# Ten exact down chunks instead of eight in two token blocks, and another split of their first parts between VectorE and ScalarE

## The chip, the cores and the metric

The kernel runs on one core of a Trainium2 chip. The metric is the device time of one execution in microseconds (us); the number to compare is the median of several runs.

## The reference

An attention with polynomial sketches is followed by a gated feed-forward block. Cut to what matters:

```python
# attention: batch 4, heads 4, sequence 1088, head size 32, sketch 8 x 8
num = einsum(q_p, einsum(k_p, v));  den = einsum(q_p, sum(k_p)) + 1e-6
x = (num / den) as (4352 tokens, 128)
# feed-forward, 1536 hidden channels
g = x @ w_gate                       # 128 x 1536
val = x @ w_val                      # 128 x 1536
out = (silu(g) * val) @ w_out        # 1536 x 128
```

All inputs come as 64-bit floats; the output is 4352 x 128 in fp32. The change lies in the last product, `@ w_out`.

## The kernel before

**Tiling.** The 1536 hidden channels are 12 chunks of 128 (`NCH`). The 4352 tokens are cut into blocks (L65 to L72): three blocks of the first batch row (384, 320 and 384 tokens), then the later blocks, six of 480 tokens and one of 384. The list of later blocks is `line` (L886), so `line[4]` and `line[5]` are the fifth and the sixth later block, and `line[6]` is the last one (`LAST`). The three first blocks and the attention fill about the first half of the span; the change lies in the second half.

**The loop of the later blocks** (L1405 to L1423) runs over all chunks of all later blocks in one row, 12 turns to a block. This document counts turns within a block: turn t is chunk t. In one turn TensorE gets, in this order: the start of the unit of the next chunk (`start_unit`, two matmuls on L989), the rest of the unit of this chunk (`finish_unit`, four matmuls on L1001 and L1002), and one down product (`down`) of a chunk five turns earlier, taken from the list `todo`.

**A unit** makes gate and value of one chunk. Both products are made in three fast fp32r matmuls each instead of one true fp32 matmul: weights and tokens have been cut beforehand into parts whose products are exact enough together. After the L989 pair, ScalarE scales both sums in place (L992, 960 columns); after the four further matmuls ScalarE makes the silu `sg` (L1004), and VectorE multiplies the value with it into the hidden chunk `hbuf` (L1009). The two sums lie in a pair of PSUM banks; there are three such pairs. The pair is let go at L1012, behind L1009, and the unit that starts three turns after starts in it. Its first L989 writes the bank of the gate, which L1004 has read, its second the bank of the value, which L1009 has read.

**The down product** (L1054) adds hidden chunk times `w_out` chunk into PSUM. For most chunks it is one plain fp32 matmul (L1077, which the profile counts as two records). For the chunks in the list `DOWN` (L888 to L890) it is three fp32r matmuls (L1069, L1071, L1072). For these the hidden chunk has to be cut into three parts as well, by `cut_hidden` (L951):

- `h1`, one turn after the chunk is made: the chunk times a constant, rounded to fp32r. By ScalarE (L968) or by VectorE (L966), as the condition on L965 says. ScalarE does it behind its own work of that turn, VectorE ahead of L1009.
- `h0`, two turns after: chunk minus `h1`, by GpSimd (L969). GpSimd does little else there, so that it starts as soon as `h1` is there.
- `hd`, three turns after: a difference by VectorE (L972), ahead of L1009 of that turn.

The dictionaries `before` and `behind` hold these steps by turn; `finish_unit` runs the first ahead of its matmuls (L998), the second after L1009 (L1013). Within a turn older steps stand first, so VectorE gets L972, then L966, then L1009. Every engine takes its instructions in the order in which the program lists them. There are six sets of the three parts' buffers, taken in turn (L960).

Chunks whose down product stays plain use a copy of `w_out` times -1 (`scaled`), whose places `PLAIN` lists (L887). It is made for chunks 0, 1, 3, 5, 7, 6 and 11; `exchange` (L934), in turn 8 of the sixth block, overwrites those of 1, 5 and 7 with 8, 9 and 10 for the last block.

**Other steps around the change.** In turns 2 and 3 of a block the tokens of the next block are cut: L865 on ScalarE, L868 on GpSimd, L873 on VectorE. In turns 4 to 6 the sums of the block before are brought together and stored: L1095 on ScalarE, L1105 and the transpose L1131 on VectorE, four or more DMAs on SP's queue.

Of the kernel before, what the change touches and what calls it, by code (L numbers as in the profile page):

```python
# [19 lines left out]
def kernel(  # L20
# [796 lines left out]
    def whole(ap):  # L817
        return ap.bitcast(FP32)
# [67 lines left out]
    line = list(range(HEAD, len(blocks)))  # L886
    FINE, PLAIN = range(1, NCH - 1), [0, 1, 3, 5, 7, 6, NCH - 1]  # L887
    DOWN = [(line[2], j) for j in (2, 4, 6, 8, 9, 10)]  # L888
    DOWN += [(i, j) for i in line[3:6] for j in (1, 2, 4, 5, 7, 8, 9, 10)]
    DOWN += [(LAST, j) for j in (1, 2, 4, 5, 6, 7)]  # L890
    down_parts = {}
    h_parts = {}
# [3 lines left out]
    def add_to(where, y, f):  # L896
        where.setdefault(y, []).append(f)
# [53 lines left out]
    def cut_hidden(y, i, j):  # L951

        if not h_sets:
            x = []
            for tag in ("kld", "qld", "vld", "kT", "qT"):
                t = const.tile([P, 2, WB], F32R, tag=tag, name="h" + tag, bufs=1)
                x += [t[:, k, :] for k in range(2)]
            t = const.tile([P, 8, WB], F32R, tag="late", name="hlate", bufs=1)
            x += [t[:, k, :] for k in range(8)]
            h_sets.extend(x[k : k + 3] for k in range(0, 18, 3))  # L960
        n = SPLIT if i == LAST else blocks[i][1]
        h_sets.append(h_sets.pop(0))
        h1, h0, hd = h_parts[i, j] = [x[:, 0:n] for x in h_sets[-1]]
        h = hidden[i, j][:, 0:n]
        if j in (2, 5, 8, 10) and i != line[2]:  # L965
            add_to(before, y + 1, lambda: nc.vector.tensor_scalar(h1, h, CUT, None, op0=ALU.mult))  # L966
        else:
            add_to(behind, y + 1, lambda: nc.scalar.activation(h1, h, AF.Copy, scale=CUT))  # L968
        add_to(before, y + 2, lambda: nc.gpsimd.tensor_tensor(  # L969
            out=h0, in0=h, in1=whole(h1), op=ALU.subtract  # L970
        ))
        add_to(before, y + 3, lambda: nc.vector.scalar_tensor_tensor(  # L972
            out=hd, in0=whole(h1), scalar=WHOLE, in1=h, op0=ALU.mult, op1=ALU.subtract
        ))
# [19 lines left out]
    def finish_unit(i, j, y=None):  # L994
        n = blocks[i][1]
        x1, x0, _ = (x[:, 0:n] for x in x_parts[i])
        ps = sums_of.pop((i, j))
        now(before, y)  # L998
        for k, w in enumerate((wg, wv)):
            w1, wb = (w_parts[id(w), j // 3][t][:, j % 3, :] for t in range(2))  # L1000
            nc.tensor.matmul(ps[:, k], w1, x1, start=False, stop=False, skip_group_check=True)  # L1001
            nc.tensor.matmul(ps[:, k], wb, x0, start=False, stop=True, skip_group_check=True)  # L1002
        sg = fpool.tile([P, WB], FP32, tag="sg", name="sg", bufs=5)[:, 0:n]
        nc.scalar.activation(sg, ps[:, 0], AF.Silu, scale=WHOLE)  # L1004
        slot_of[i, j] = slots.pop(0)
        hj = slot_of[i, j]
        hidden[i, j] = hj
        todo.append((i, j))
        nc.vector.scalar_tensor_tensor(  # L1009
            out=hj[:, 0:n], in0=ps[:, 1], scalar=WHOLE, in1=sg, op0=ALU.mult, op1=ALU.mult  # L1010
        )
        let_go((i, j))  # L1012
        now(behind, y)  # L1013
        if (i, j) in DOWN:
            cut_hidden(y, i, j)
# [451 lines left out]
```

## Time and profile before

| what | value |
|---|---|
| median of 3 runs | 277.68 us (277.06 to 278.61) |
| the profiled execution: its time | 276.96 us |
| the profiled execution: its span | 275.2 us |
| granted TensorE clock | 0.998 |
| TensorE matmul, busy | 98% of the span |
| VectorE, busy | 76% |
| ScalarE, busy | 70% |
| GpSimd, busy | 37% |
| fifth later block (204.4 to 228.8 us): TensorE, VectorE, ScalarE, GpSimd busy | 24.40, 20.54, 20.24, 11.39 us |

In the profile "PE" is TensorE's matmuls, "PEld" its weight loads, "DVE" VectorE, "ACT" ScalarE, "POOL" GpSimd, and L1009 is line 1009 of the kernel. A timeline row gives the start in us from the begin of the span, the duration in us, the engine, the line, the operation, and output and input; in square brackets stands how long the engine sat idle before it, and who released it. The span is shorter than the execution's time by 1.76 us, which lie around it.

### The profile page before, as it was taken

The numbers are of one execution on the slowest core, as the hardware profiler recorded it, in microseconds if no ns is written. First come the engines' busy times: TensorE is split into PE (matmuls) and PEld (weight loads), VectorE is DVE, ScalarE is ACT, GpSimd is POOL, SyncE is SP. The second block draws the span as 40 slices with busy tenths as digits, with TensorE's granted clock in tenths as the row PEclk, the third lists the DMA queues.
The fourth block names the chain that finished last, engine by engine and source line by source line (L and its number), as shares of the span: only waits on it lengthen the run. The fifth ranks groups of instructions, "written<-read, shape, count | busy, mean of one in ns | idle before, by whom it ended". The sixth has DMA issues, their size and how long they took to land.

```text
span 275.2 us, 5762 instructions
## 1 busy us (share of the span) xinstructions
PE 269.1 (98%) x2187; PEld 199.8 (73%) x2187; DVE 209.7 (76%) x369; ACT 191.9 (70%) x345; POOL 101.0 (37%) x113
## 2 busy tenths in 40 slices
PE   7899999999999999999999999999999999999995
PEld 7645566666785777777577777867887888788994
DVE  3997988989798773887545666967977995978771
ACT  3468566372685686677478898768879878897880
POOL 3314422159250630260043353435425553543320
PEclk9999999999999999999999999999999999999999
DMA  6673196222231043000200020000100200010021
GB/s 192 171 225 90 35 277 194 77 87 77 48 92 18 4 113 98 2 0 1 38 13 4 4 36 0 0 2 12 25 2 0 36 1 0 15 23 1 5 33 29
DMA packets 26139, 14.30 MB, mean 52 GB/s; under 512 B 19840, under 2 KB 24192, under 8 KB 26112
## 3 DMA queue, kind: packets, MB, share of 16 engines
q1 hardware_dynamic: 25456, 13.84, 19.5%
q8 instruction: 17, 0.28, 0.4%
q10 hardware_dynamic: 656, 0.10, 0.2%
q14 instruction: 10, 0.08, 0.1%
HBM read 11.41 MB, written 2.23 MB: 50 GB/s over the span
## 4 chain that ended last, share of the span: by engine, by line
PE 93%; DVE 3%; DMA 2%; ACT 1%; issue 0%; SPq 0%
PE PS L1077 21%; PE PS L1001 14%; PE PS L989 14%; PE PS L1002 14%; PE PS L1025 12%; PE PS L1072 3%; PE PS L1069 3%; PE PS L1071 3%; PE PS L354 2%; PE PS L776 2%; PE PS L342 2%; PE PS L388 2%; DMA kld<-in_k_dram 2%; PE PS L1117 1%; PE PS L497 1%; PE PS L445 1%
## 5 line engine op out<-in xcount | busy, mean ns | idle before, releaser
L992 ACT ACTIVATE PS<-PS 128x960 f32<-128x960 f32 (+1 forms) x90 | 83.3, 926 | 31.9 <-PE PS L989 31.0
L1009 DVE SCALAR_TENSOR_TENSOR hbuf<-PS,sg 128x480 f32<-128x480 f32 (+1 forms) x87 | 55.3, 636 | 41.1 <-ACT sg L1004 39.0
L1004 ACT ACTIVATE sg<-PS 128x480 f32<-128x480 f32 (+1 forms) x90 | 49.6, 551 | 1.6 <-PE PS L1002 1.2
L1077 PE MATMUL PS<-hbuf,wo 128*128 128x480 f32 (+2 forms) x94 | 39.4, 516 | 0.0
L989 PE MATMUL PS<-xd,graw 128*128 128x480 f32 (+1 forms) x69 | 37.7, 546 | 0.0
L989 PE MATMUL PS<-xd,wd 128*128 128x480 f32 (+1 forms) x90 | 33.5, 372 | 0.0
L1002 PE MATMUL PS<-x,wb 128*128 128x480 f32 (+1 forms) x90 | 33.5, 372 | 0.0
L1001 PE MATMUL PS<-x,w 128*128 128x480 f32 (+1 forms) x90 | 33.4, 371 | 0.0
L1002 PE MATMUL PS<-x,graw 128*128 128x480 f32 (+1 forms) x69 | 25.5, 370 | 0.0
L989 PEld LDWEIGHTS PS<-xd,wd 128*128 128x128 f32 x90 | 17.0, 189 | 10.3 <-issue 5.8
L1025 PE MATMUL PS<-xT,wg 128*128 128x384 f32 (+1 forms) x60 | 23.5, 474 | 0.1
L1025 PE MATMUL PS<-xT,wv 128*128 128x384 f32 (+1 forms) x60 | 23.2, 467 | 0.3 <-DVE wv L286 0.3
L1077 PEld LDWEIGHTS PS<-hbuf,wo 128*128 128x128 f32 x94 | 17.6, 189 | 5.4 <-issue 0.4
L868 POOL TENSOR_TENSOR x<-xT,x 128x480 fp32r<-128x480 f32 (+1 forms) x6 | 7.2, 1192 | 38.1 <-ACT x L865 38.1
L1077 PE MATMUL PS<-hbuf,scaled 128*128 128x480 f32 (+1 forms) x48 | 20.6, 518 | 0.0
L1029 ACT ACTIVATE sg<-PS 128x384 f32<-128x384 f32 (+1 forms) x24 | 11.2, 468 | 13.2 <-PE PS L1025 12.3
L989 PEld LDWEIGHTS PS<-xd,graw 128*128 128x128 f32 x69 | 13.0, 188 | 7.7 <-ACT PS L992 4.1
L969 POOL TENSOR_TENSOR hlate<-hbuf,hlate 128x480 fp32r<-128x480 f32 (+1 forms) x12 | 14.3, 1198 | 11.3 <-ACT hlate L968 9.2
L1001 PEld LDWEIGHTS PS<-x,w 128*128 128x128 f32 x90 | 16.9, 187 | 2.2
L1002 PEld LDWEIGHTS PS<-x,wb 128*128 128x128 f32 x90 | 16.9, 188 | 2.1
L1001 PE MATMUL PS<-x,graw 128*128 128x480 f32 (+1 forms) x48 | 18.0, 376 | 0.0
L1025 PEld LDWEIGHTS PS<-xT,wv 128*128 128x128 f32 x60 | 11.2, 190 | 7.3 <-DVE hbuf L1040 0.8
(203 smaller groups left out, 555.2 us busy)
## 6 DMA issues: line engine op xcount, KB each, us to landing
kld<-in_k_dram SPq DMA_DIRECT2D x4, 544.0 KB, 4.2
vld<-in_v_dram SPq DMA_DIRECT2D x12, 144.0 KB, 4.0
qld<-in_q_dram SPq DMA_DIRECT2D x3, 544.0 KB, 4.9
raw<-in_moe_w_out_dram SPq DMA_DIRECT2D x4, 384.0 KB, 4.3
raw<-in_moe_w_gate_dram SPq DMA_DIRECT2D x3, 384.0 KB, 3.6
raw<-in_moe_w_val_dram SPq DMA_DIRECT2D x3, 384.0 KB, 3.8
out_dram<-o SPq DMA_DIRECT2D x16, 60.0 KB, 2.0
vld<-in_v_dram SPq DMA_DIRECT2D x4, 112.0 KB, 3.9
```

The source lines that it names most:

```text
L969: add_to(before, y + 2, lambda: nc.gpsimd.tensor_tensor(out=h0, in0=h, in1=whole(h1), op=ALU.subtract))
L989: nc.tensor.matmul(ps[:, k], w_parts[id(w), j // 3][2][:, j % 3, :], xd, start=True, stop=True)
L992: nc.scalar.activation(ps, ps, AF.Copy, scale=-1.0 / WHOLE)
L1001: nc.tensor.matmul(ps[:, k], w1, x1, start=False, stop=False, skip_group_check=True)
L1002: nc.tensor.matmul(ps[:, k], wb, x0, start=False, stop=True, skip_group_check=True)
L1004: nc.scalar.activation(sg, ps[:, 0], AF.Silu, scale=WHOLE)
L1009: nc.vector.scalar_tensor_tensor(out=hj[:, 0:n], in0=ps[:, 1], scalar=WHOLE, in1=sg, op0=ALU.mult, op1=ALU.mult)
L1025: nc.tensor.matmul(o[:, 0:n], w[:, j, :], xT[:, t0 : t0 + n], start=True, stop=True)
L1029: nc.scalar.activation(sg[:, 0:n], g[:, 0:n], AF.Silu)
L1069: nc.tensor.matmul(acc[i][:, 0:n], wd, hd, **sides)
L1071: nc.tensor.matmul(p, w1, h1, start=(j == mine[0]), stop=False)
L1077: nc.tensor.matmul(acc[i][:, 0:n], w, hidden[i, j][:, 0:n], **sides)
```

## The change

Two lines change. In the fifth and the sixth later block (`line[4]` and `line[5]`) all of chunks 1 to 10 (`FINE`) get exact down products; before, chunks 3 and 6 were plain. The fourth later block keeps its eight. The condition that says which engine makes `h1` changes for these two blocks: VectorE makes it for chunks 3, 6, 7, 8, 9 and 10, ScalarE for 1, 2, 4 and 5; before, VectorE had 2, 5, 8 and 10 and ScalarE 1, 4, 7 and 9. The last block and the fourth keep the old split.

```diff
     DOWN = [(line[2], j) for j in (2, 4, 6, 8, 9, 10)]
-    DOWN += [(i, j) for i in line[3:6] for j in (1, 2, 4, 5, 7, 8, 9, 10)]
+    DOWN += [(i, j) for i in line[3:6] for j in ((1, 2, 4, 5, 7, 8, 9, 10) if i == line[3] else FINE)]
     DOWN += [(LAST, j) for j in (1, 2, 4, 5, 6, 7)]
...
         h = hidden[i, j][:, 0:n]
-        if j in (2, 5, 8, 10) and i != line[2]:
+        if j in ((3, 6, 7, 8, 9, 10) if i in line[4:6] else (2, 5, 8, 10)) and i != line[2]:
             add_to(before, y + 1, lambda: nc.vector.tensor_scalar(h1, h, CUT, None, op0=ALU.mult))
         else:
             add_to(behind, y + 1, lambda: nc.scalar.activation(h1, h, AF.Copy, scale=CUT))
```

The rows of instructions in the changed program: TensorE 8 matmuls more (12 more of the exact kind, 4 plain ones less), VectorE 8 more, ScalarE the same number, GpSimd 4 more; SP's queue is the same.

## The prediction

> **What bounds the kernel now.** I read the totals first, then the chain of waits, then the timelines of TensorE, of its weight loads, of VectorE and of GpSimd around the two blocks concerned.
>
> ```profile
> PE 269.1 (98%) x2187; PEld 199.8 (73%) x2187; DVE 209.7 (76%) x369; ACT 191.9 (70%) x345; POOL 101.0 (37%) x113
> PE 93%; DVE 3%; DMA 2%; ACT 1%; issue 0%; SPq 0%
> ```
>
> TensorE is the chain: 93% of it. So a part taken from TensorE is gained in full, as long as nothing makes TensorE wait. The TensorE timeline gives the price of one turn of the loop over chunks. I measure a turn from one second L989 matmul to the next.
>
> ```profile
> 206.64 0.38 PE L989 MATMUL PS<-xd,wd 128*128 128x480 f32 x1
> ...
> 208.59 0.38 PE L989 MATMUL PS<-xd,wd 128*128 128x480 f32 x1
> ...
> 209.67 0.97 PE L1077 MATMUL PS<-hbuf,scaled 128*128 128x480 f32 x2
> ...
> 210.69 0.38 PE L989 MATMUL PS<-xd,wd 128*128 128x480 f32 x1
> ```
>
> A turn with the three exact parts takes 208.59 - 206.64 = 1.95, a turn with a plain down chunk (L1077) 210.69 - 208.59 = 2.10. All turns from 188 to 245 us take 1.95 to 1.97 or 2.10 to 2.12: TensorE has no gap there. VectorE has far less room:
>
> ```profile
> 209.47 1.03 DVE L873 SCALAR_TENSOR_TENSOR xd<-x,xT 128x480 fp32r<-128x480 f32 x1
> 210.42 1.67 DVE L972 SCALAR_TENSOR_TENSOR hqT<-hkT,hbuf 128x480 fp32r<-128x480 f32 x1
> 212.02 0.65 DVE L1009 SCALAR_TENSOR_TENSOR hbuf<-PS,sg 128x480 f32<-128x480 f32 x1
> 212.58 0.64 DVE L972 SCALAR_TENSOR_TENSOR hlate<-hqT,hbuf 128x480 fp32r<-128x480 f32 x1
> 213.15 0.64 DVE L1105 SCALAR_TENSOR_TENSOR sum<-PS,sum 128x480 f32<-128x480 f32 x1
> 213.72 0.64 DVE L1009 SCALAR_TENSOR_TENSOR hbuf<-PS,sg 128x480 f32<-128x480 f32 x1
> ```
>
> The L1009 of turn 4 starts at 212.02, though ScalarE's L1004 had its `sg` ready at 210.43 (start 209.87, 0.56 long). L1009 sets the PSUM pair free that the unit three later starts in, and the weight loads show that this one was just in time:
>
> ```profile
> 212.72 0.19 PEld L989 LDWEIGHTS PS<-xd,wd 128*128 128x128 f32 x1 [0.34 <-DVE hbuf L1009]
> ```
>
> So the second L989 of turn t+2 (here at 212.81) comes no earlier than 0.79 after L1009 of turn t starts. In turn 4 of the fifth later block there is nothing left to use up.
>
> **What the Trainium skill says.** "FP8 and Floating Point Precision", TensorE Precision Notes: true fp32 takes four passes through the array. That agrees: the chain has 0.81 for a plain chunk, and three parts lie 0.217 apart, 0.65 together. "SBUF — State Buffer", Who interferes with whom: a VectorE instruction with two SBUF inputs, or in a two-port mode, shares a port pair with GpSimd as an exclusive lock; whoever is second waits for the whole of the other. That agrees: L972 (inputs `h1` and `h`, both in SBUF) takes 0.64 alone and up to 1.71 beside a GpSimd L969, and L966 takes 0.36 to 0.41 or 1.28. L1009, with one input in PSUM, keeps 0.64 to 0.66 always. "TensorE: Matmul & The Clock Gate", Step-by-step: what each phase is for: matmuls stay in program order, only weight loads are pulled ahead. So a late L1009 stops all of TensorE; the 0.34 above is the only sight of it here.
>
> ```profile
> 224.92 0.40 DVE L966 TENSOR_SCALAR hqT<-hbuf 128x480 fp32r<-128x480 f32 x1
> 225.24 0.64 DVE L1009 SCALAR_TENSOR_TENSOR hbuf<-PS,sg 128x480 f32<-128x480 f32 x1
> 225.81 1.40 DVE L972 SCALAR_TENSOR_TENSOR hqT<-hkT,hbuf 128x480 fp32r<-128x480 f32 x1
> 227.13 0.64 DVE L1009 SCALAR_TENSOR_TENSOR hbuf<-PS,sg 128x480 f32<-128x480 f32 x1
> ```
> ```profile
> 225.46 1.24 POOL L969 TENSOR_TENSOR hlate<-hbuf,hqT 128x480 fp32r<-128x480 f32 x1 [0.98 <-DVE hqT L966]
> ```
>
> This is the lock at work. L966 makes `h1`; 0.54 after its start GpSimd takes L969 and holds the pair to 226.70. VectorE does L1009 meanwhile, then L972 has to wait, and the next instruction starts 0.43 after GpSimd ends. One round L966, L1009, L972 is 2.20 us (224.92 to 227.13 is 2.21; 200.75 to 202.95 gives 2.20 too), longer than TensorE's 1.95.
>
> **The change part by part.** Turn t is chunk t of a block (t12 and more lie in the next); down of chunk t comes five turns later.
>
> *TensorE.* Chunks 3 and 6 of the fifth and the sixth later block become exact: four plain chunks less, twelve matmuls more. 4 x 0.15 = 0.60 us saved, all on the path.
>
> *ScalarE.* Four L968 per block before and after, but now of chunks 1, 2, 4, 5. Chunk 2's (0.49 from start to start) falls into turn 3, right behind L865, and makes `sg` of turn 4 some 0.2 late. Nothing: L1009 of turn 4 waits 1.6 us for VectorE anyway. Without that cover it would cost up to 0.2 per block. Later turns lose work there.
>
> *GpSimd.* Two L969 more per block, 4 x 1.24 in all. It was busy 11.4 of 24.4 us in the fifth block, so its own queue costs nothing; its lock counts, below. SP's queue and the DMAs stay as they were.
>
> *VectorE.* Per block two L972 and two L966 more, and L966 moves to chunks 3, 6, 7, 8, 9, 10. From the order of the changed program: turn 4 has L972(1), L966(3), L1009; turn 5 L972(2), L1105, L1009; turn 6 L972(3), L1131, L1009; turns 7 to 11 each L972, L966, L1009. Behind each of these wait L1009, then TensorE. I walk the queue with the starts of before.
>
> Fifth block, turn 4: L966(3) starts at 212.02 and takes 0.30 (224.92 to 225.24, and 214.87 to 215.16 elsewhere), so L1009 starts at 212.32, and the second L989 of turn 6 is at 213.11 instead of 212.81: 0.30 lost. Turn 5: L966(3) releases GpSimd at 212.54, which holds the pair to 213.78; L972(2), free before, now ends at 214.21. Then L1105 0.57, so L1009 is at 214.78 (before 213.72), the L989 of turn 7 at 215.57 instead of 214.78: 0.79 lost so far. Turn 6: L972(3), L1131, L1009 at 216.5; limit for it 215.57 + 1.95 - 0.79 = 216.7. Turn 7: L972(4) waits for GpSimd's chunk 5, then L966(6); L1009 at 218.06, limit 218.7. From here a round takes 2.20 and TensorE wants one each 1.95. L1009 of turns 8 to 11: 220.26, 222.46, 224.66, 226.86; limits 220.64, 222.60, 224.55, 226.50. Turn 10 loses 0.11, turn 11 another 0.25. Then no more L966, and VectorE recovers in two turns. Sum for the block 1.15.
>
> Sixth block: L1009 of turn 4 was at 235.85 with the L989 of turn 6 at 236.93, so L966 costs 0.01. Turn 5: GpSimd holds 236.37 to 237.61, L972 ends 238.04, L1105 238.61, + 0.79 = 239.40 against 238.89: 0.51. The dense turns go as above, but the next block is narrower (turns of 1.71 from 248.87), so the limits come closer: L1009 of turns 10, 11, 12 at about 248.5, 250.7, 252.6 lose 0.25, 0.49, 0.05. Sum 1.30.
>
> Sum: 1.15 + 1.30 - 0.60 = +1.85. The profiled execution took 276.96 (span 275.2 and 1.76 around it); that gives 278.8. The median of the runs is 277.68, 0.72 above it, so the forecast is 277.68 + 1.85 = 279.5.
>
> Bounds of what the trace doesn't show. The stall itself: below zero is excluded, a wait gives nothing back; at least nothing, if the lock falls otherwise. At most: the L989 comes 0.9 after L1009 (a whole weight load of 0.19 after its end) and not 0.79, some 0.1 at each of five stalls; a round of 2.25 adds 0.05 in ten turns; ScalarE 0.2 twice: +1.4. I take the values of the walk, since each has a twin in this trace.
>
> **The rivals.**
> - *VectorE binds in both places* (above): 279.5, 0.52.
> - *Only chunk 3 binds.* In turns 8 to 11 L972 gets the pair ahead of GpSimd whenever L1009 waits for `sg`; then a round fits into 1.95, and only 0.79 + 0.51 is lost: +0.7, 278.4. For it: 219.40 to 224.92 VectorE is never over 0.1 behind `sg`. Against: it enters the run late. 0.25.
> - *TensorE has the room* (the other side: not slower). Three PSUM pairs cover a late L1009 by about 1.2 us; if the inserted L966 finds that room, the 0.60 is kept: 277.1. It decides at 212.02 + 0.79: it needs L1009 of turn 4 to come earlier than before, as L966(2) is gone from turn 3. Against: VectorE idled 1.16 in turn 3 after that L966. 0.10.
> - *Lateness feeds on itself*: the upper bounds hold, 280.9. 0.13.
> - That the exact chunks aren't made is no case: the order shows eight more matmuls.
>
> **How the numbers follow.** About 0.5% (1.4 us) can be told from no change. Slower by more: 0.47 of the first case and all of the last, 0.60. Within: 0.05 of the first, 0.25, and 0.07 of the third, 0.37. Faster by more: 0.03. Range: 277.8 leaves out the third case (0.10), 281.2 takes in the last.
>
> **What would show it.** Right: weight loads of L989 that wait for VectorE L1009 in turns 6 and 7 of both blocks, 0.8 and 0.5 together, and in the last turns; parts turns of 1.95 elsewhere; L972(2) of about 1.3 instead of 0.64. Wrong: no such waits, and turns 8 and 11 simply 0.15 shorter; or L972 in turns 8 to 11 of 0.64.

## The result, and the profile after

| what | before | after |
|---|---|---|
| median of 6 runs | 277.25 us | 279.23 us |
| ratio, 95% interval | | 1.007 [1.0049, 1.0091] |
| the profiled execution: time, span | 276.96, 275.2 us | 279.47, 277.7 us |

The changed kernel is slower by 1.98 us, where +1.85 was forecast. As a time, 279.5 was forecast: the median of three that it started from was 0.43 above the median of six. Of the 2.5 us between the two spans, 0.47 lie ahead of anything that was changed: the second L989 of turn 2 of the fifth block stands at 204.68 before and at 205.15 after. That place differs by up to 0.5 between the profiled executions of kernels that are the same up to there. From there to turn 4 of the last block (255.72 and 258.25) the difference grows by 2.06.

First the page of the changed kernel, busy times and the chain:

```profile
PE 269.9 (97%) x2191; PEld 199.7 (72%) x2191; DVE 214.8 (77%) x377; ACT 191.8 (69%) x345; POOL 106.5 (38%) x117
...
PE 90%; DVE 5%; DMA 2%; issue 1%; ACT 1%; SPq 0%; DVEq 0%
```

VectorE gained two points in the chain, though its busy share rose by only one. The place shows in VectorE's timeline, turns 4 and 5 of the fifth block (start, duration):

```profile
212.49 0.40 DVE L966 TENSOR_SCALAR hlate<-hbuf 128x480 fp32r<-128x480 f32 x1
212.81 0.65 DVE L1009 SCALAR_TENSOR_TENSOR hbuf<-PS,sg 128x480 f32<-128x480 f32 x1
213.37 1.39 DVE L972 SCALAR_TENSOR_TENSOR hlate<-hqT,hbuf 128x480 fp32r<-128x480 f32 x1
214.68 0.65 DVE L1105 SCALAR_TENSOR_TENSOR sum<-PS,sum 128x480 f32<-128x480 f32 x1
215.25 0.64 DVE L1009 SCALAR_TENSOR_TENSOR hbuf<-PS,sg 128x480 f32<-128x480 f32 x1
```

Against the rows of before that the prediction shows, L966 of chunk 3 is new, and the L972 behind it takes 1.39 in place of 0.64. TensorE's weight loads show who waits for that. In brackets stands how long the weight load sat idle, which is more than TensorE lost: turns 5 and 6 are 0.25 and 0.68 longer than their 2.10 and 1.95.

```profile
213.50 0.19 PEld L989 LDWEIGHTS PS<-xd,wd 128*128 128x128 f32 x1 [0.66 <-DVE hbuf L1009]
...
215.38 0.19 PEld L1071 LDWEIGHTS PS<-hkT,dparts 128*128 128x128 f32 x1 [0.71 <-DVE sum L1105]
```

The second waiter is one that the prediction did not name: the first L1071 of a block writes the PSUM bank that L1105 has to read out before. Both L1105 and L1009 had become late together.

Then the run of five rounds, on VectorE and on GpSimd:

```profile
220.56 0.40 DVE L966 TENSOR_SCALAR hkT<-hbuf 128x480 fp32r<-128x480 f32 x1
220.88 0.65 DVE L1009 SCALAR_TENSOR_TENSOR hbuf<-PS,sg 128x480 f32<-128x480 f32 x1
221.45 1.41 DVE L972 SCALAR_TENSOR_TENSOR hvld<-hqld,hbuf 128x480 fp32r<-128x480 f32 x1
222.78 0.40 DVE L966 TENSOR_SCALAR hqT<-hbuf 128x480 fp32r<-128x480 f32 x1
```
```profile
221.10 1.24 POOL L969 TENSOR_TENSOR hkT<-hbuf,hkT 128x480 fp32r<-128x480 f32 x1 [0.98 <-DVE hkT L966]
```

A round lasts 222.78 - 220.56 = 2.22; GpSimd ends at 222.34, and only then does L972 end. At the end of the run TensorE waits again, here and once more at 228.22:

```profile
226.02 0.19 PEld L989 LDWEIGHTS PS<-xd,wd 128*128 128x128 f32 x1 [0.35 <-DVE hbuf L1009]
```

### The profile page after: what moved, and what is told of

Same layout as the page of the kernel before. It is cut to its first block, busy times and chain, and to the rows that moved or that the text cites. A ratio compares the mean times of both kernels' runs of the same rounds, so it can differ in the third digit from the quotient of the medians.

```text
span 277.7 us, 5791 instructions
## 1 busy us (share of the span) xinstructions
PE 269.9 (97%) x2191; PEld 199.7 (72%) x2191; DVE 214.8 (77%) x377; ACT 191.8 (69%) x345; POOL 106.5 (38%) x117
## 3 DMA queue, kind: packets, MB, share of 16 engines
HBM read 11.41 MB, written 2.23 MB: 49 GB/s over the span
## 4 chain that ended last, share of the span: by engine, by line
PE 90%; DVE 5%; DMA 2%; issue 1%; ACT 1%; SPq 0%; DVEq 0%
PE PS L1077 19%; PE PS L989 14%; PE PS L1001 13%; PE PS L1002 13%; PE PS L1025 12%; PE PS L1071 3%; PE PS L1072 3%; PE PS L1069 3%; PE PS L354 2%; PE PS L776 2%; PE PS L342 2%; DMA kld<-in_k_dram 2%; PE PS L388 2%; PE PS L1117 1%; PE PS L497 1%
## 5 line engine op out<-in xcount | busy, mean ns | idle before, releaser
L992 ACT ACTIVATE PS<-PS 128x960 f32<-128x960 f32 (+1 forms) x90 | 83.4, 926 | 32.6 <-PE PS L989 31.9
L1009 DVE SCALAR_TENSOR_TENSOR hbuf<-PS,sg 128x480 f32<-128x480 f32 (+1 forms) x87 | 55.2, 634 | 38.6 <-ACT sg L1004 36.7
L989 PE MATMUL PS<-xd,graw 128*128 128x480 f32 (+1 forms) x69 | 36.9, 535 | 0.0
L989 PE MATMUL PS<-xd,wd 128*128 128x480 f32 (+1 forms) x90 | 34.1, 379 | 0.3 <-DVE hbuf L1009 0.2
L1001 PE MATMUL PS<-x,w 128*128 128x480 f32 (+1 forms) x90 | 33.4, 371 | 0.0
L989 PEld LDWEIGHTS PS<-xd,wd 128*128 128x128 f32 x90 | 17.0, 188 | 11.8 <-issue 5.1
L969 POOL TENSOR_TENSOR hlate<-hbuf,hlate 128x480 fp32r<-128x480 f32 (+1 forms) x12 | 14.4, 1204 | 13.2 <-ACT hlate L968 8.6
L1001 PEld LDWEIGHTS PS<-x,w 128*128 128x128 f32 x90 | 16.9, 187 | 2.2
L989 PEld LDWEIGHTS PS<-xd,graw 128*128 128x128 f32 x69 | 13.0, 188 | 7.3 <-ACT PS L992 3.2
L1001 PE MATMUL PS<-x,graw 128*128 128x480 f32 (+1 forms) x48 | 18.0, 376 | 0.0
L1077 PE MATMUL PS<-hbuf,scaled 128*128 128x480 f32 (+1 forms) x40 | 16.8, 508 | 0.0
```

Source lines behind the costliest of these rows:

```text
L969: add_to(before, y + 2, lambda: nc.gpsimd.tensor_tensor(out=h0, in0=h, in1=whole(h1), op=ALU.subtract))
L989: nc.tensor.matmul(ps[:, k], w_parts[id(w), j // 3][2][:, j % 3, :], xd, start=True, stop=True)
L992: nc.scalar.activation(ps, ps, AF.Copy, scale=-1.0 / WHOLE)
L1009: nc.vector.scalar_tensor_tensor(out=hj[:, 0:n], in0=ps[:, 1], scalar=WHOLE, in1=sg, op0=ALU.mult, op1=ALU.mult)
L1077: nc.tensor.matmul(acc[i][:, 0:n], w, hidden[i, j][:, 0:n], **sides)
```

## The experiments

The theory: GpSimd's L969 holds a port pair against L972, so a round with L966 in it takes 2.2 us, and VectorE falls behind TensorE in turns 4 to 5 and 7 to 11. The rivals: exact chunks cost this wherever their first part is made; VectorE simply has too many instructions. Below, "against before" is the difference of medians, measured on the same chip; the kernels in which a step was put on other lines have their later line numbers shifted by one (L1009 is L1010 there).

**The chunks alone**, with the old split:

```diff
-        if j in ((3, 6, 7, 8, 9, 10) if i in line[4:6] else (2, 5, 8, 10)) and i != line[2]:
+        if j in (2, 5, 8, 10) and i != line[2]:
```

> The ten exact chunks, but the old split of the first parts: VectorE makes those of 2, 5, 8, 10, ScalarE those of 1, 3, 4, 6, 7, 9. Lock theory (a round of L966, L1009, L972 beside GpSimd's L969 lasts 2.2 us): no two rounds with L966 follow each other, turns 8 to 12 lose at most 0.3 per block; turn 5 loses about 0.3, as GpSimd's chunk 3 still stands in the way of L972. Together with the 0.60 saved: +0.2 against before, between -0.4 and +0.8. Rival, that exact chunks cost this wherever their first part is made: +1.5 to +2.0, as the changed kernel.

Measured: 277.09 against 277.17, ratio 0.9995 [0.9981, 1.0008]. The loss is gone with the split, so the exact chunks themselves don't make it. But the 0.60 is not kept either. The waits of the weight loads in the two blocks (total, times, longest):

```profile
PEld PS L989 <- DVE hbuf L1009: 1.0, 4, 0.4
...
PEld PS L1071 <- DVE sum L1105: 0.6, 2, 0.4
```

Turn 6 of the fifth block still takes 2.28 in place of 1.95, and the last turns of the sixth are 0.05 to 0.1 too long each.

**The split alone**: before, with the new condition on L965 and the old list `DOWN`.

> The new split (VectorE makes the first parts of 7, 8, 9, 10), but chunks 3 and 6 plain as before. Lock theory: in turn 4 no L966, in turn 9 no L972, so that VectorE enters the dense turns on time and catches up in turn 9: no wait of over 0.1, within 0.3 of before. Rival, that four first parts in a row on VectorE are enough for the loss: +0.7 to +1.2, all in turns 10 to 12.

Measured: 277.27 against 277.17, ratio 1.0001 [0.9984, 1.0018]. Four first parts in a row on VectorE cost nothing here. VectorE's timeline says why:

```profile
221.33 0.71 DVE L972 SCALAR_TENSOR_TENSOR hqld<-hkld,hbuf 128x480 fp32r<-128x480 f32 x1
...
222.72 0.66 DVE L1009 SCALAR_TENSOR_TENSOR hbuf<-PS,sg 128x480 f32<-128x480 f32 x1 [0.37 <-ACT sg L1004]
223.30 0.95 DVE L972 SCALAR_TENSOR_TENSOR hvld<-hqld,hbuf 128x480 fp32r<-128x480 f32 x1
...
224.67 0.66 DVE L1009 SCALAR_TENSOR_TENSOR hbuf<-PS,sg 128x480 f32<-128x480 f32 x1
225.25 1.22 DVE L972 SCALAR_TENSOR_TENSOR hqT<-hkT,hbuf 128x480 fp32r<-128x480 f32 x1
```

L972 grows by about 0.25 from turn to turn, which is the difference of a round and a TensorE turn, and L1009's idle time shrinks from 0.37 to none. VectorE came in on time, and the run ended when its headroom was used up. So a run of rounds has a price only beyond its headroom. And neither half of the change makes the loss: the ten exact chunks alone don't, the new split alone doesn't, only both together do.

**Without h0**: L969 left out in the two blocks.

```diff
-        add_to(before, y + 2, lambda: nc.gpsimd.tensor_tensor(
-            out=h0, in0=h, in1=whole(h1), op=ALU.subtract
-        ))
+        if i not in line[4:6]:
+            add_to(before, y + 2, lambda: nc.gpsimd.tensor_tensor(
+                out=h0, in0=h, in1=whole(h1), op=ALU.subtract
+            ))
```

> The changed kernel without GpSimd's L969 (h0) in the fifth and the sixth block; the matmul that reads h0 gets what lies in its buffer. VectorE's work stays as it is. Lock theory: L972 takes 0.64 everywhere in the two blocks, a round 0.57 + 0.57 + 0.30 = 1.44, no weight load waits for L1009 or L1105; only the 0.60 saved is left: -0.6 against before. Rival, that VectorE has too many instructions there, lock or not: at least half of the loss stays, +0.7 or more.

Measured: 276.53 against 277.17, -0.64, ratio 0.9968 [0.9955, 0.998]. This is the run that separates lock from load: VectorE has every instruction of the changed kernel, and the whole loss is gone. One of its groups by shape (busy, mean ns; L973 is L972 of the other kernels); the other groups of L973 have 648 to 650 ns too:

```profile
L973 DVE SCALAR_TENSOR_TENSOR hqT<-hkT,hbuf 128x480 fp32r<-128x480 f32 x4 | 2.6, 650 | 0.0
```

The changed kernel has, for the same group, and up to 1495 ns for the others:

```profile
L972 DVE SCALAR_TENSOR_TENSOR hqT<-hkT,hbuf 128x480 fp32r<-128x480 f32 x4 | 5.1, 1276 | 0.0
```

**L1105 ahead of L972 in turn 5**:

```diff
-            add_to(before, y + 1, join)
+            before.setdefault(y + 1, []).insert(0, join)
```

> The changed kernel, but L1105 stands ahead of L972 in turn 5. It has one input in SBUF and one in PSUM, and so needs no lock: it should run while GpSimd holds the pair, at no cost. Lock theory with turn 5 as read after the change: L1071 no longer waits for L1105 (0.7 in each block), L1009 of turn 5 comes 0.57 earlier, turns 6 and 7 take 1.95; the losses of turns 10 to 12 stay. 1.2 less than the changed kernel: +0.8 against before. Rival, that turn 5 is lost because of L1009 in any case: at most 0.2 less than the changed kernel.

Measured: 278.49 against 277.17, +1.32, ratio 1.0042 [1.003, 1.0054]. Better than the changed kernel by about 0.66, half of what I expected. The waits for L1105 are gone, and turn 6 takes 2.05 and 1.97 in the two blocks, not 2.63 and 2.51. But the waits for L1009 are now:

```profile
PEld PS L989 <- DVE hbuf L1009: 3.4, 9, 0.7
```

against 2.7 in 7 waits in the changed kernel. In the fifth block L972 of chunk 3, free in the changed kernel at 0.64, now takes 1.11 beside GpSimd, turns 7 and 8 lose 0.05 and 0.11, turn 11 0.15 in place of 0.10. What TensorE no longer lost in turn 6, 1.12 in the two blocks, VectorE had no time to work off: some 0.4 of it was given back later.

**Chunk 3's first part on ScalarE**, the others as in the changed kernel: `(6, 7, 8, 9, 10) if i in line[4:6]`.

> The changed kernel, but ScalarE makes the first part of chunk 3 in the two blocks; VectorE makes those of 6 to 10. Theory (turn 5 is lost because L966 of chunk 3 stands in turn 4, turns 10 to 12 because of five rounds in a row): turns 6 and 7 lose no more than with the old split, 0.33 and 0.04, and turns 10 to 12 lose what they did after the change, 0.45 and 0.8. +1.0 against before, between +0.6 and +1.3. Rival, that the backlog of VectorE is one and what is saved in turn 5 is given back in turns 10 to 12: +1.5 or more. Rival, that five rounds in a row cost nothing when VectorE enters them on time: +0.1 or less.

Measured: 278.10 against 277.27, +0.83, ratio 1.0029 [1.0016, 1.0041]. So taking L966 of chunk 3 off VectorE is worth 1.98 - 0.83 = 1.15. Most of what stays lost lies at the end of the five rounds: turns 11 to 13 of the fifth block still take 2.04, 2.20 and 2.08. Not all of it does: turn 6 still takes 2.23, 0.28 too long, where the old split had 2.28.

**GpSimd fills h0 with zeros**: `nc.gpsimd.memset(whole(h0), 0.0)` in the two blocks in place of the subtraction.

> The changed kernel, but GpSimd fills h0 with zeros in the fifth and the sixth block and does not compute it: the same queue and nearly the same times, but it reads nothing from SBUF. If the lock is for reads alone, as the Trainium skill has it for an instruction with two SBUF inputs: L972 takes 0.64 beside it, L966 may still wait for it; as without h0, -0.6 to -0.3. Rival, that any GpSimd instruction holds the pair against L972: L972 still over 1 us, +1.0 or more, as far as the fill lasts over 1 us.

Measured: 276.63 against 277.27, ratio 0.9976 [0.9962, 0.9989], with L972 at 0.63 to 0.65 throughout the two blocks. The expectation goes by the Trainium skill, "SBUF — State Buffer", Who interferes with whom. In the dense turns this decides nothing: a fill takes 0.50, waits only for TensorE, and lies almost wholly beside L1009, which never waited for GpSimd. But around turns 3 and 4 of both blocks the fills follow one another without a gap, beside L972 and L966. GpSimd's timeline and VectorE's:

```profile
209.44 1.38 POOL L969 MEMSET hlate<- 128x480 f32 x3
210.76 0.49 POOL L969 MEMSET hkld<- 128x480 f32 x1
```
```profile
210.29 0.65 DVE L972 SCALAR_TENSOR_TENSOR hqT<-hkT,hbuf 128x480 fp32r<-128x480 f32 x1
210.86 1.10 DVE L966 TENSOR_SCALAR hlate<-hbuf 128x480 fp32r<-128x480 f32 x1
233.90 0.65 DVE L972 SCALAR_TENSOR_TENSOR hqld<-hkld,hbuf 128x480 fp32r<-128x480 f32 x1
```

L972 at 210.29 runs wholly beside fills and takes its 0.65; so does the one at 233.90 (three fills from 233.83 to 235.47). The same L972 beside GpSimd's subtraction takes 1.67 in the changed kernel. L966 behind it does wait: 1.10, and 0.56 at 234.47, in place of 0.40. So a GpSimd instruction that only writes held up L966 but not L972, in two places of one trace, as the page has it.

**The old split with L1105 first**, the change of `join` above and `(2, 5, 8, 10)` in all blocks; and **an alternating split with L1105 first**, `(3, 6, 8, 10)` in the two blocks:

> Ten exact chunks in the two blocks, the old split of first parts (VectorE 2, 5, 8, 10), and L1105 ahead of L972 in turn 5. The old split alone lost 0.33 in turn 7 of the fifth block to L1071 waiting for L1105 and 0.3 at the end of the sixth. Theory: the first goes, the second stays: -0.35 against before, between -0.6 and -0.1. Rival, that the backlog is given back later: no better than the old split alone, -0.1.

> As the run before, but VectorE makes the first parts of 3, 6, 8, 10 in the two blocks. Theory: L966 of chunk 3 in turn 4 costs 0.25 in the fifth block once more, and rounds with and without L966 alternate from turn 7, so that turns 10 to 12 lose at most 0.2: 0.0 against before, between -0.3 and +0.4. Rival, that only five in a row matter, -0.4 or less.

Measured: the first 277.02 against 277.27, ratio 0.9984 [0.9973, 0.9996]; the second 277.41 against 277.27, ratio 0.9999 [0.9983, 1.0015]. In the first one's trace the 0.33 of turn 6 is 0.05, but turns 7 and 8 take 2.10 and 2.07. From turn 6 to turn 14 it needs 15.97 us, with the old split alone 15.96: all given back, as the rival said, and its median may be no better than that of the old split alone. In the second, turn 5 loses 0.25 to L966 of chunk 3 once more, and turns 11 to 13 of the fifth block none: the alternation does what was expected of it, but turns 5 to 8 and the last turns of the sixth block (0.07 to 0.10 each) lose what the exact chunks save.

**h0 on VectorE**, first parts of 2, 8, 9 on VectorE and the rest on ScalarE:

```diff
-        if j in ((3, 6, 7, 8, 9, 10) if i in line[4:6] else (2, 5, 8, 10)) and i != line[2]:
+        if j in ((2, 8, 9) if i in line[4:6] else (2, 5, 8, 10)) and i != line[2]:
...
-        add_to(before, y + 2, lambda: nc.gpsimd.tensor_tensor(
+        engine = nc.vector if i in line[4:6] else nc.gpsimd
+        add_to(before, y + 2, lambda: engine.tensor_tensor(
```

> Ten exact chunks in the two blocks, h0 made by VectorE (0.57 from start to start) and not by GpSimd, the first parts by ScalarE but for chunks 2, 8, 9. No GpSimd instruction of these blocks then stands against L972. Lock theory: a round of L1009, L972, h0 is 3 x 0.57 = 1.71, less than TensorE's 1.95, though VectorE has more instructions than in the changed kernel; no weight load waits for VectorE by over 0.1, and the 0.60 is kept: -0.6 against before, between -0.8 and -0.2 (ScalarE may lose some). Rival, that the number of VectorE instructions decides: +1 or more.

Measured: 276.58 against 277.17, -0.59, ratio 0.9978 [0.9971, 0.9986]. This version computes all that the changed kernel does and is faster than both kernels. VectorE (L970 is h0):

```profile
220.10 0.64 DVE L973 SCALAR_TENSOR_TENSOR hvld<-hqld,hbuf 128x480 fp32r<-128x480 f32 x1
220.67 0.65 DVE L970 TENSOR_TENSOR hkT<-hbuf,hkT 128x480 fp32r<-128x480 f32 x1
221.23 0.40 DVE L966 TENSOR_SCALAR hqT<-hbuf 128x480 fp32r<-128x480 f32 x1
221.55 0.64 DVE L1010 SCALAR_TENSOR_TENSOR hbuf<-PS,sg 128x480 f32<-128x480 f32 x1
222.12 0.64 DVE L973 SCALAR_TENSOR_TENSOR hqT<-hkT,hbuf 128x480 fp32r<-128x480 f32 x1
```

From one L973 to the next it takes 2.02 with all four steps in it, less than the 2.22 of three steps beside GpSimd; without L966 1.70 (218.40 to 220.10). All turns of the two blocks take their 1.95 or 2.10.

**The same in the fourth block too**, with ten exact chunks there (`line[3:6]` in both places, and `FINE` for all three):

> The same in the fourth, fifth and sixth block, with ten exact chunks in each: two plain chunks less, 0.30 more saved. -0.9 against before, between -1.1 and -0.3. Rival, that the fourth block, whose turns 2 to 4 hold attention steps too, runs late: no better than the run before, -0.6 or less of a gain.

Measured: 277.06 against 277.17, ratio 1.0002 [0.9985, 1.0019]. The rival was right that the fourth block is the trouble, and the engine that is late there is ScalarE. Its timeline in turns 4 and 5:

```profile
185.74 0.59 ACT L968 ACTIVATE hkT<-hbuf 128x480 fp32r<-128x480 f32 x1
186.23 0.56 ACT L1096 ACTIVATE sum<-PS 128x480 f32<-128x480 f32 x1
186.68 0.97 ACT L993 ACTIVATE PS<-PS 128x960 f32<-128x960 f32 x1
```

The added L968 stands ahead of L993, for which TensorE's weight load sits idle for 0.84 and TensorE itself for 0.44; one turn takes 2.80, 2.33 in the run before. That is 0.47 lost for 0.30 saved, 0.17 of the 0.48 by which this run is behind the one before. The rest lies outside the span: the times of this run are about 2.08 above their spans, 1.72 in the run before and in the kernel before. Why is not known. I did not try to move this one first part to VectorE.

## Why the prediction was right, point by point

- *TensorE is the chain, 0.15 saved for each of four chunks.* Right: with the lock taken away the kernel gains 0.64 (without h0) or 0.59 (h0 on VectorE), where 0.60 was worked out.
- *The rule of 0.79 from L1009 to the L989 behind it.* Right, though the records seem to say 0.70 (212.81 to 213.51):

```profile
212.81 0.39 PE L989 MATMUL PS<-xd,wd 128*128 128x480 f32 x1
213.04 0.37 PE L1001 MATMUL PS<-x,graw 128*128 128x480 f32 x1
```
```profile
213.51 0.48 PE L989 MATMUL PS<-xd,wd 128*128 128x480 f32 x1
213.83 0.38 PE L1001 MATMUL PS<-x,graw 128*128 128x480 f32 x1
```

  In the second pair TensorE had stood still: its L989 is recorded together with the weight load that waited (213.50), 0.48 long and not 0.39, and the matmul behind it follows after 0.32 in place of 0.23. The L1001 behind stands 1.02 after the start of L1009 in both kernels: 212.02 to 213.04 before, 212.81 to 213.83 after. So some 0.10 of a loss read from L989 to L989 shows one turn late.
- *The walk through VectorE's queue.* Its losses, by turns. Measured is how much longer a turn is than its 1.95 or 2.10, for this reason from one L1001 behind the second L989 to the next; at the end of the sixth block, than the same turn before, less 0.15 where a plain chunk went:

| place | walk | measured |
|---|---|---|
| fifth block, L966 of chunk 3 | 0.30 | 0.35 |
| fifth block, L972 behind GpSimd | 0.49 | 0.57 |
| fifth block, end of the five rounds | 0.11, 0.25, 0 | 0.21, 0.24, 0 |
| sixth block, chunk 3 | 0.01, 0.50 | 0.02, 0.57 |
| sixth block, end of the five rounds | 0.25, 0.49, 0.05 | 0.25, 0.48, 0.05 |

  Over whole stretches, from L989 to L989: turn 2 to turn 14 grew from 24.13 to 25.13, and from there to turn 28 from 26.91 to 27.97, in each with 0.30 saved: 1.30 and 1.36 lost, 1.15 and 1.30 forecast. (Turns of before are up to 0.02 longer than 1.95 and 2.10, so the table adds up to a little more.)
- *Who waits in turn 5.* Here the working had a gap. I listed L1009 and TensorE's L989 behind it, but not what waits for L1105 itself, the first L1071 of the block. It waited first, so that no L989 of turn 7 waits, and added about 0.10 in each block: that L989 stands at 216.14 and 240.93, where 0.79 after L1009 would be 216.04 and 240.83. The time came out near because both are late for one reason, and they are about as far apart on TensorE as on VectorE. That they are was luck: nothing in the working looked at it.
- *A round of 2.20.* Measured 2.22. The run began later than walked: L1009 of turn 7 stands at 218.67, on the clock of before 218.20 and not 218.06. That and the 0.02 of each round, less the 0.10 that L1071 had already cost TensorE, make the 0.21 in place of 0.11.
- *ScalarE's queue costs nothing.* Nothing in the trace speaks against it: no weight load in the two blocks waited for L992.
- *The rivals.* "Only chunk 3 binds" falls: with its L966 taken off, +0.83 stayed, and the waits at the end of the rounds with it. Its reason was half right, though. The split alone shows that four rounds in a row are free when VectorE enters them on time. "TensorE has the room" falls with the first wait. "Lateness feeds on itself" falls: each round of the run took 2.20 to 2.22, no more. The runs with L1105 first showed the other side of that: what is saved early is partly or wholly lost later, as VectorE's backlog is one.

## What to carry to other kernels

When TensorE is full and a helper's queue is nearly full, don't count the helper's busy time, walk its queue through the turns, with the real durations of each neighbour, and list everything that waits for each instruction that becomes late. An instruction that is cheap alone can be the first of a chain through a shared port: look for one form that shows two durations in the trace. Then more instructions on one engine can be faster than fewer on two that block each other.

## What the runs showed of the hardware

- GpSimd and VectorE as helpers of each other can be slower than VectorE alone: `h0` takes 1.24 on GpSimd and 0.65 on VectorE, and on GpSimd it holds up an L972 of 0.65 to 1.41 meanwhile. In the stretch from turn 2 to turn 27 VectorE ran 63 instructions in the changed kernel and 77 with `h0` on it, and the second kernel was the faster.
- What GpSimd does decides who waits: beside its subtraction L972 took up to 1.68, beside its fills 0.65, while L966 beside fills took 1.10 and 0.56 in place of 0.40.
- TensorE's weight load follows within 0.04 to 0.06 of the end of the VectorE instruction that it waits for (213.46 to 213.50, 225.96 to 226.02), and the matmul behind the waiting one comes 0.32 after it, where it is 0.22 or 0.23 without a wait (213.51 to 213.83; 212.81 to 213.04 before).
- An L972 that is blocked has its next instruction 0.43 to 0.44 after GpSimd ends (222.34 to 222.78), not the 0.57 that it needs from start to start when free. What becomes of the other 0.13 is not shown.
